# Broadcasts of source indices cut into pieces of 112, 8 and 8 partitions

## The chip, the core and the metric

The kernel runs on one core of one Trainium2 chip. The metric is the device time of one execution in microseconds, as the median of several runs. Beside it stands one execution that was taken with the hardware profiler; all views of a profile come from that one.

## The reference

One GraphSAGE layer over a random graph: 12,500 nodes with 64 features, 800,000 edges, and for each node the sum of the features of the nodes that point to it, scaled by the inverse of its degree.

```python
def reference(x, src, dst, deg_inv, w_self, w_neigh):
    N = x.shape[0]
    nsum = _segment_sum(x[src], dst, N)
    h_neigh = nsum * deg_inv[:, None]
    return x @ w_self + h_neigh @ w_neigh
```

`src` and `dst` are uniform random integers, so every node has about 64 edges, and which ones is known only at run time.

## The kernel before, in words

The kernel has no gather of single rows over the 800,000 edges. It sorts the edges into buckets on the chip and turns both the gather and the segment sum into matmuls with one-hot matrices.

**Sorting (until about 1100 us).** Each edge becomes one 32-bit key of the block of its destination (144 nodes, two halves of 72), the block of its source (128 nodes), and its places within the two. VectorE sorts 128 runs of 6,250 keys, GpSimd gathers pieces of the runs with indirect DMAs, VectorE merges them, and the result is cut into 87 x 98 = 8,526 buckets of 128 slots, one for each pair of destination and source block. This is done in two parts: 128 rows of 41 buckets first, then 128 rows of 27 (`KPRS`). The merges, the search and the decoding of the second part (lines 272 to 324, 606, 655 and 672 to 726 among others) run beside the node stage until about 1670 us. Decoding leaves two tables: `sl` in DRAM, a row of 128 bf16 source places for each bucket, and `dlT` in SBUF, the destination places, slots on the partitions.

**The node stage (`nodes`, from 1098 us to 2176 us).** All that the change touches lies here. The 8,526 buckets are taken in order, in tiles of 8:

- `one_hots` (line 770) makes the one-hot matrices for 28 buckets at a time, 305 times. A broadcast DMA from SyncE's queue (line 777) copies the 28 rows of `sl`, 7,168 bytes in one piece, to each of the 128 partitions of the tile `slb`; so a broadcast is 128 rows of 7 KB, 896 KB. VectorE compares it with the partition's number (line 779), which gives `ohs`: for each bucket a matrix of 128 source nodes by 128 slots. Line 782 compares `dlT` with 0 to 71 and gives `ohd`, slots by destinations.
- `gather` (line 798): for each bucket TensorE multiplies `ohs` with the features of the source block, `xh` (two f16 halves of each number, 128 columns), into PSUM (`ct`, line 807): the features of the 128 edges of the bucket. ScalarE copies a tile of 8 buckets to SBUF as f16 (`xg`, line 817); from tile 540 on every second one is VectorE's where the one-hots are far enough ahead (line 815).
- `sums` (line 826): TensorE multiplies `xg` with `ohd` into one of two accumulators (`acc`, line 863), 64 slots at a time. This is the segment sum. It runs two or three tiles behind `gather`.
- Every 7 destination blocks the accumulators are copied out (`g`), multiplied with `w_neigh` (`po`, line 931), scaled, added to the self terms (`fo`, an ACT-queue load of 126 partitions) and stored (`out`, GpSimd's queue). A few edges that fit in no bucket come from indirect DMAs (`lx`, line 844).

What sets the order: the loops run under a manual schedule, so each engine gets its instructions in the order in which the code is written. `gather` fetches one-hots until 44 buckets lie ahead (`AHEAD`). The tiles `slb` and `ohs` have 3 buffers each, `ohd` 6, `xg` 7 and `ct` 3: SyncE issues a broadcast when VectorE's compare has freed the buffer three broadcasts back, and the compare waits for the landing of its broadcast and for TensorE to be done with an `ohs` three back. Each DMA from SyncE or ScalarE takes one of eight completion semaphores in turn (`DMAHW0` to `DMAHW7`), and one that comes to a semaphore whose last DMA may still be under way waits for that.

The self terms, the check of the leftovers and the general path (lines 941 to 1016, which runs only if the buckets overflow) play no part in what follows.

Of the kernel before, what the change touches and what calls it, by code (L numbers as in the profile page):

```python
# [335 lines left out]
class Kernel:  # L336
# [433 lines left out]
    def one_hots(self, pool):  # L770


        nc = self.nc
        for c in range(0, NBID, 28):
            b = pool.tile([128, 28 * 128], BF, name="slb", bufs=3)
            src = self.sl[c:c + 28]
            nc.sync.dma_start(b, bass.AP(tensor=src.tensor, offset=src.offset, ap=[[0, 128], [1, 28 * 128]]))
            s = pool.tile([128, 28, 128], FH, name="ohs", bufs=3)
            nc.vector.tensor_scalar(s.rearrange("p c s -> p (c s)"), b, self.pidx[:, :1], None, op0=OP.is_equal)  # L779
            d = pool.tile([128, 14, HN, 2], FH, name="ohd", bufs=6)  # L780
            ix = self.dlT[:, c:c + 28].rearrange("p (c t) -> p c t", t=2)[:, :, None, :].to_broadcast([128, 14, HN, 2])
            nc.vector.tensor_tensor(d, self.iota[:, None].to_broadcast([128, 14, HN, 2]), ix, op=OP.is_equal)  # L782
            yield [(s[:, j], d[:, j // 2, :, j % 2]) for j in range(28)]
# [376 lines left out]
```

## Time and profile before

| | us |
|---|---|
| median of three runs | 2203.3 |
| the three runs | 2197.75, 2203.3, 2210.69 |
| the profiled execution | 2187.6 |
| its span, first to last instruction | 2185.9 |
| start of the first broadcast | 1098.1 |
| last broadcast issued | 2160.9 |
| mean granted TensorE clock | 0.769 |

Names in a profile: PE is TensorE's matmul, PEld its load of weights, DVE is VectorE, ACT ScalarE, POOL GpSimd, SP SyncE; L807 is line 807 of the kernel, and `ct<-xh,ohs` a result and its operands by the program's names. A row of the waits reads "engine, tile and line that waited <- who ended it: us in total, times, the longest". "issue" there means that the engine stood and nothing that the profile shows held it. The chain of waits is followed back from the last instruction: at each step to what released it, or to the instruction before it on its engine. A window is a stretch of the span in us. A DMA queue's row gives its packets, its megabytes, and the time that its packets took as a share of 16 DMA engines' span.

### The profile page before, as it was taken

Reading aid. Unit: us, or ns where it says so; the run is one execution under the profiler, and the core shown is the slowest. Engines: PE = TensorE matmul, PEld = TensorE weight load, DVE = VectorE, ACT = ScalarE, POOL = GpSimd, SP = SyncE. Lnnn points to the kernel's source line nnn. Section 1 sums busy time; section 2 is a strip of 40 time slices with the busy share of each in tenths; the row PEclk is TensorE's granted clock in tenths of the full one; section 3 lists DMA queues with packets and bytes.
Section 4 is the critical chain, followed back from the end, with each engine's and each line's share of the span. In section 5 each row is a group of like instructions: output and inputs, shape, how many; then the busy total and the mean of one; then the engine's idle time right before and its main releaser. Section 6 shows DMA issues by size and latency. Waiting matters only on the chain.

```text
span 2185.9 us, 59793 instructions
## 1 busy us (share of the span) xinstructions
PE 1026.7 (47%) x26089; PEld 885.7 (41%) x26089; DVE 1997.1 (91%) x2193; ACT 1263.6 (58%) x1743; POOL 648.6 (30%) x1016
## 2 busy tenths in 40 slices
PE   0050000000000000000068998999987989999888
PEld 0050000000000000000067887878776877788777
DVE  7899999999899599988999999999998988898887
ACT  6470000009700000062269999999998888898887
POOL 0000000000888888977771101011340110100110
PEclk9975555555555555555589999999999999999999
DMA  5140000001000000011177787777876787787785
GB/s 162 29 107 11 0 0 0 0 7 53 21 20 19 18 13 14 10 50 51 47 271 263 269 293 265 280 262 281 309 275 232 274 288 281 264 312 280 272 284 177
DMA packets 111471, 331.46 MB, mean 152 GB/s; under 512 B 57008, under 2 KB 65136, under 8 KB 110560
## 3 DMA queue, kind: packets, MB, share of 16 engines
q1 hardware_dynamic: 74127, 299.80, 37.0%
q0 software_dynamic: 14736, 18.99, 4.9%
q10 hardware_dynamic: 22337, 8.76, 1.8%
q8 instruction: 206, 3.38, 0.6%
q14 instruction: 65, 0.53, 0.1%
HBM read 308.39 MB, written 19.10 MB: 150 GB/s over the span
## 4 chain that ended last, share of the span: by engine, by line
PE 36%; DVE 33%; POOL 10%; issue 9%; ACT 8%; DMA 2%; ACTq 1%; another core or an unknown queue 0%; DVEq 0%; POOLq 0%; SPq 0%
PE ct L807 21%; PE acc L863 14%; DVE a L228 9%; DVE b L228 9%; POOL u L467 6%; DVE u L292 6%; ACT xg L817 3%; POOL pad L382 2%; ACT junka L448 2%; DVE u L324 2%; DMA v<-d,ix 1%; POOL v L625 1%; PE po L931 1%; DVE u L280 1%; ACT junk L604 1%
## 5 line engine op out<-in xcount | busy, mean ns | idle before, releaser
L817 ACT ACTIVATE xg<-ct 128x1024 f16<-128x1024 f32 (+1 forms) x994 | 939.1, 1091 | 99.2 <-PE ct L807 79.1
L807 PE MATMUL ct<-xh,ohs 128*128 128x128 f16 x8526 | 600.7, 221 | 58.0 <-issue 24.6
L807 PEld LDWEIGHTS <-ohs 128*128 128x128 f16 x8526 | 496.5, 99 | 104.7 <-issue 44.1
L467 POOL DMA_INDIRECT u<-d,ix x256 | 336.0, 1313 | 543.4 <-ACT junka L448 500.8
L292 DVE TENSOR_TENSOR u<-u 128x256 f32<-128x256 f32 (+47 forms) x494 | 452.8, 947 | 23.1 <-ACT u L276 15.7
L863 PE MATMUL acc<-ohd,xg 64*128 64x72 f16 x17052 | 410.1, 194 | 49.2 <-issue 35.1
L863 PEld LDWEIGHTS <-xg 64*128 64x128 f16 x17052 | 323.9, 94 | 124.6 <-issue 45.7
L779 DVE TENSOR_SCALAR ohs<-slb,pidx 128x3584 f16<-128x3584 bf16 x305 | 350.1, 1148 | 20.3 <-PE ct L807 17.1
L782 DVE TENSOR_TENSOR ohd<-iota,dlT 128x2016 f16<-128x2016 bf16 x305 | 365.8, 1199 | 0.0
L692 PE MATMUL tr<-idb,l 128*128 128x128 bf16 x68 | 9.0, 271 | 492.5 <-ACT l L686 487.6
L228 DVE TENSOR_TENSOR b<-a 128x106 f32<-128x106 f32 (+36 forms) x112 | 227.3, 2080 | 10.3 <-ACT a L231 9.3
L228 DVE TENSOR_TENSOR a<-b 128x106 f32<-128x106 f32 (+31 forms) x114 | 228.5, 2056 | 1.2
L276 ACT ACTIVATE u<-u 128x256 f32<-128x256 f32 (+15 forms) x94 | 47.3, 589 | 309.7 <-DVE u L280 308.3
L692 PEld LDWEIGHTS <-l 128*128 128x128 bf16 x68 | 5.6, 116 | 496.0 <-ACT l L686 491.4
L457 PE MATMUL stp<-idf,st 128*128 128x128 f32 x2 | 0.9, 446 | 420.4 <-DVE st L455 420.4
L939 POOL DMA_DIRECT2D out<-o x24 | 24.3, 1014 | 540.0 <-DVE o L938 470.6
L457 PEld LDWEIGHTS stp<-idf,st 128*128 128x128 f32 x2 | 0.4, 183 | 420.9 <-issue 420.9
L844 POOL DMA_INDIRECT lx<-xt,lxi x44 | 80.0, 1818 | 297.9 <-DVE lxi L842 181.0
L815 DVE CAST xg<-ct 128x1024 f16<-128x1024 f32 x75 | 91.6, 1222 | 58.1 <-PE ct L807 57.7
L231 ACT ACTIVATE a<-b 128x106 f32<-128x106 f32 (+12 forms) x20 | 13.5, 710 | 218.8 <-DVE b L228 195.2
L382 POOL MEMSET pad<- 128x89 f32 x594 | 114.6, 193 | 17.4
L625 POOL DMA_INDIRECT v<-d,ix x68 | 85.3, 1254 | 53.4 <-ACT ix L655 19.2
(134 smaller groups left out, 846.5 us busy)
## 6 DMA issues: line engine op xcount, KB each, us to landing
slb<-sl SPq DMA_DIRECT2D x305, 896.0 KB
u<-d,ix POOLq DMA_INDIRECT x256
xt<-xh SPq DMA_DIRECT2D x1, 3136.0 KB
own<-os SPq DMA_DIRECT2D x12, 256.0 KB
fo<-own ACTq DMA_DIRECT2D x24, 126.0 KB
out<-o POOLq DMA_DIRECT2D x24, 126.0 KB
rd<-dst SPq DMA_DIRECT2D x5, 521.0 KB
rs<-src SPq DMA_DIRECT2D x5, 521.0 KB
```

The source lines that it names most:

```text
L228: nc.vector.tensor_tensor(view(dst, lo + sh, [[st, g], [1, l]]), x, y, op=op)
L292: nc.vector.tensor_tensor(to, at(cur, ln + lo, n), at(cur, lo + k, n), op=op)
L382: self.nc.gpsimd.memset(self.pad, 0.0)
L467: nc.gpsimd.indirect_dma_start(out=u[:nr, p * w:(p + 1) * w], out_offset=None, in_=src, in_offset=bass.IndirectOffsetOnAxis(ap=self.start[ ...
L625: self.nc.gpsimd.indirect_dma_start(out=self.v[:, k].bitcast(F32), out_offset=None, in_=flat(self.d2[part], 128 * PITCH2[part]), in_offset ...
L779: nc.vector.tensor_scalar(s.rearrange("p c s -> p (c s)"), b, self.pidx[:, :1], None, op0=OP.is_equal)
L782: nc.vector.tensor_tensor(d, self.iota[:, None].to_broadcast([128, 14, HN, 2]), ix, op=OP.is_equal)
L807: nc.tensor.matmul(ct[:, i * 128:(i + 1) * 128], cols[i][0], self.xh[:, (b0 + i) % NB].rearrange("p a f -> p (a f)"), start=True, stop=True)
L815: nc.vector.tensor_copy(xg[:, :cnt * 128], ct[:, :cnt * 128])
L817: nc.scalar.activation(xg[:, :cnt * 128], ct[:, :cnt * 128], AF.Copy)
L844: nc.gpsimd.indirect_dma_start(out=x, out_offset=None, in_=self.xt, in_offset=bass.IndirectOffsetOnAxis(ap=ix.bitcast(U32), axis=0))
L863: nc.tensor.matmul(acc[h][:, db % OCT * HN:(db % OCT + 1) * HN], xg[r, i * 128:(i + 1) * 128], d[r], start=db % OCT == 0 and sb == 0, stop ...
```

## The change

Each broadcast is issued as three DMAs: one to partitions 0 to 111, one to 112 to 119 and one to 120 to 127. They read the same 7 KB and write the same tile. As the change is described, some DMA engines then get 9 of the 128 rows and the others 7, where each had 8.

```diff
         for c in range(0, NBID, 28):
             b = pool.tile([128, 28 * 128], BF, name="slb", bufs=3)
             src = self.sl[c:c + 28]
-            nc.sync.dma_start(b, bass.AP(tensor=src.tensor, offset=src.offset, ap=[[0, 128], [1, 28 * 128]]))
+            for p, n in ((0, 112), (112, 8), (120, 8)):
+                nc.sync.dma_start(b[p:p + n], bass.AP(tensor=src.tensor, offset=src.offset, ap=[[0, n], [1, 28 * 128]]))
             s = pool.tile([128, 28, 128], FH, name="ohs", bufs=3)
             nc.vector.tensor_scalar(s.rearrange("p c s -> p (c s)"), b, self.pidx[:, :1], None, op0=OP.is_equal)
```

The order on PE, DVE, ACT and POOL is the same in both programs; lines behind 777 are numbered one higher. On SP 305 rows become 915. The broadcasts of the first chunks as they stand on SP before, from the second and third of the stage on, each with the semaphores that it waits for (DVE frees the buffer, DMAHW is a landing):

```order
L777 DMA slb<-sl 128x3584 x2
L777 DMA slb<-sl 128x3584 [waits DMAHW0_49,DVE_49]
L777 DMA slb<-sl 128x3584 [waits DMAHW1_49,DVE_49]
L777 DMA slb<-sl 128x3584 [waits DMAHW2_49,DVE_49]
L777 DMA slb<-sl 128x3584 [waits DMAHW3_49,DVE_49]
L777 DMA slb<-sl 128x3584 [waits DMAHW4_49,DVE_49]
```

And the same place now, from the third broadcast on:

```order
L778 DMA slb<-sl 112x3584
L778 DMA slb<-sl 8x3584
L778 DMA slb<-sl 8x3584 [waits DMAHW0_49]
L778 DMA slb<-sl 112x3584 [waits DMAHW2_49,DMAHW1_49,DVE_49]
L778 DMA slb<-sl 8x3584
L778 DMA slb<-sl 8x3584 [waits DMAHW3_49]
L778 DMA slb<-sl 112x3584 [waits DMAHW5_49,DMAHW4_49,DVE_49]
L778 DMA slb<-sl 8x3584 [waits DMAHW6_49]
L778 DMA slb<-sl 8x3584 [waits DMAHW7_49]
```

The large piece waits for the buffer as the whole broadcast did; the small ones follow it at once, but mostly wait for the landing of the DMA that had their semaphore, eight issues before. On DVE the compare stands where it stood, with other waits. Before, between the merges of the second part (`u`) early in the node stage:

```order
L779 TENSOR_SCALAR ohs<-slb,pidx 128x3584 [waits DMAHW2_49,PE_49]
L782 TENSOR_TENSOR ohd<-iota,dlT 128x2016
L292 TENSOR_TENSOR u<-u 128x734
L292 TENSOR_TENSOR u<-u 128x736 [waits DVE_49]
L779 TENSOR_SCALAR ohs<-slb,pidx 128x3584 [waits DMAHW4_49,PE_49]
```

And the same rows now:

```order
L780 TENSOR_SCALAR ohs<-slb,pidx 128x3584 [waits DMAHW3_49,DMAHW4_49,DMAHW2_49,PE_49]
L783 TENSOR_TENSOR ohd<-iota,dlT 128x2016
L292 TENSOR_TENSOR u<-u 128x734
L292 TENSOR_TENSOR u<-u 128x736 [waits DVE_49]
L780 TENSOR_SCALAR ohs<-slb,pidx 128x3584 [waits DMAHW6_49,DMAHW7_49,DMAHW0_49,PE_49]
```

The compare waits for three landings in place of one; nothing else moved.

## The prediction

> **What bounds the kernel now.** I read the page first, for the DMA queues and the instruction counts. The queues' rows give packets, megabytes and the share of 16 engines' span that the packets took.
>
> ```profile
> span 2185.9 us, 59793 instructions
> PE 1026.7 (47%) x26089; PEld 885.7 (41%) x26089; DVE 1997.1 (91%) x2193; ACT 1263.6 (58%) x1743; POOL 648.6 (30%) x1016
> q1 hardware_dynamic: 74127, 299.80, 37.0%
> q0 software_dynamic: 14736, 18.99, 4.9%
> q10 hardware_dynamic: 22337, 8.76, 1.8%
> q8 instruction: 206, 3.38, 0.6%
> q14 instruction: 65, 0.53, 0.1%
> slb<-sl SPq DMA_DIRECT2D x305, 896.0 KB
> ```
>
> The broadcasts are most of the traffic: 305 x 896 KB = 279.8 MB of q1's 299.80 MB (93.3%). q1 took 37.0% of 16 x 2185.9 us, which is 12,940 us of engine time; 93.3% of it, over 305 x 128 = 39,040 rows of 7 KB, is 0.31 us a row. The other reading is of q8, "instruction": 206 packets of 16.4 KB. PE and PEld together have 52,178 instructions, so a packet is 253 of them at 64.8 bytes, and the remaining 7,615 instructions fit q14 in the same way (70 bytes each). I take q8 as PE's own program, fetched in blocks; a block took 0.6% x 16 x 2185.9 / 206 = 1.02 us.
>
> The changed line works only in the node stage, from 1098 us on. I cut it at 1670 us, where the last of the sorting work that DVE does beside it is over, and asked for the busy times of the two windows (each engine's us, with its instructions in brackets).
>
> ```profile
> core 0: us, PE busy (x) PEld busy (x) DVE busy (x) ACT busy (x) POOL busy (x), PEclk, DMA share, GB/s
> 1098.00:1670.00 572.00, 517.00 (x13227) 443.29 (x13227) 547.19 (x647) 536.79 (x637) 132.75 (x99) 0.97 0.78 275
> 1670.00:2176.00 506.00, 462.54 (x12626) 405.16 (x12626) 444.17 (x505) 433.35 (x468) 49.46 (x39) 0.99 0.77 275
> ```
>
> DMA is busy 77 to 78% as a mean of 16 engines, so bandwidth as such is not used up. PE is at 90% and 91%, DVE at 96% and 88%, ACT at 94% and 86%. No engine is full in the second window, so something outside them makes them wait. The waits of the second window name it:
>
> ```profile
> ACT xg L817 <- PE ct L807: 63.2, 110, 3.2
> DVE xg L815 <- PE ct L807: 52.8, 47, 4.2
> PE acc L863 <- issue: 20.1, 22, 2.3
> PE ct L807 <- issue: 15.8, 15, 3.1
> ```
>
> ACT and DVE wait for PE; PE waits for "issue", for nothing that the profile shows: 20.1 + 15.8 = 35.9 us in 37 waits, which is 83% of the 43.5 us that PE is idle in this window (506.00 less 462.54). One such wait in the timeline (start, length, and in brackets the idle time before it):
>
> ```profile
> 1874.67 0.70 PE L863 MATMUL acc<-ohd,xg 64*128 64x72 f16 x32
> 1875.30 0.40 PE L807 MATMUL ct<-xh,ohs 128*128 128x128 f16 x4
> 1878.78 0.84 PE L807 MATMUL ct<-xh,ohs 128*128 128x128 f16 x12 [3.08 <-issue]
> 1879.21 1.22 DVE L815 CAST xg<-ct 128x1024 f16<-128x1024 f32 x1 [4.25 <-PE ct L807]
> 1879.72 1.03 ACT L817 ACTIVATE xg<-ct 128x1024 f16<-128x1024 f32 x1 [3.19 <-PE ct L807]
> ```
>
> PE stops in the middle of a tile's sixteen matmuls, after four, with its operands there, and goes on 3.08 us later; DVE and ACT then show 4.25 and 3.19 us of waiting for it. A stop inside a run of equal matmuls, together with a program that comes in blocks of 253 instructions, I read as a block that had not arrived. That such a wait sets the end is shown by the chain of waits, cut to the second window:
>
> ```profile
> by line: PE ct L807 47.5%; PE acc L863 30.5%; issue 9.3%; PE po L931 2.3%; DVE xg L815 2.3%; DVE ohd L782 1.9%; DVE ohs L779 1.9%; ACT xg L817 1.9%; PE acc L868 1.7%; DVE o L937 0.3%; DVE ltop L726 0.2%; DVE g L873 0.1%; DVE o L938 0.1%; DV
> ```
>
> It runs through PE's matmuls and 9.3% of it is issue, 47 us. DVE and ACT are about 2% each per line. In the first window DVE has the merges beside this work, and there the waits and the chain say:
>
> ```profile
> ACT xg L817 <- PE ct L807: 15.9, 21, 2.8
> PE acc L863 <- issue: 15.0, 14, 2.7
> PE ct L807 <- issue: 8.8, 10, 1.6
> ```
> ```profile
> by line: PE ct L807 38.2%; PE acc L863 24.6%; issue 11.9%; ACT xg L817 11.5%; PE po L931 1.6%; DMA slb<-sl 1.2%; PE acc L868 1.2%; DVE ohd L782 1.2%; ACT u L276 1.1%; DMA d<-u 1.1%; DVE ohs L779 1.0%; ACT l L686 0.6%; ACT ix L655 0.6%; POOL
> ```
>
> Issue is 15.0 + 8.8 = 23.8 us in 24 waits. PE's two lines are 62.8% of that chain and issue 11.9%, but ACT's copies have 11.5%, so I let three quarters of what PE gains there reach the end.
>
> **The change part by part.** Each broadcast of 28 buckets is one DMA of 128 rows now, and becomes three of 112, 8 and 8. Bytes, tiles and buffers stay, and so does the order on PE, DVE, ACT and POOL. The split, as the change is described, gives some engines nine rows of each broadcast and the others seven.
>
> *The rows on one engine.* At 0.31 us a row, an engine now works 8 x 0.31 = 2.48 us on a broadcast; with seven rows 2.17 us, with nine 2.79 us. The issues of a broadcast are 3.50 us apart, from these rows ((2160.9 - 1098.1) / 304):
>
> ```profile
> L777 SPq DMA_DIRECT2D slb<-sl x305: 319/320/427, 1098.1 to 2160.9; - x153
> L779 DVE TENSOR_SCALAR ohs<-slb,pidx x305: 1127/1145/1335, 1102.6 to 2169.7; 128x3584 f16<-128x3584 bf16 x153
>   DMA slb<-sl: 2.7, 3
> ```
>
> That fills an engine to 71%, 62% or 80%. The two windows hold 2 x (13,227 + 12,626) = 51,706 PE and PEld instructions, 204 blocks in 1078 us, so a fetch of 1.02 us comes every 5.3 us; if all lie on one engine, they fill 19% more of it. With the broadcast's rows such an engine is at 90% now, 81% with seven rows and 99% with nine. A fetch that arrives while the engine works through its rows has to wait for them, and at 90% it mostly will.
>
> *What that is worth.* I take the fetch to get in when the engine has finished its share of one DMA. The longest waits of PE, 3.1 us, fit that: share and fetch together are 2.48 + 1.02 = 3.5 us, less whatever lead the fetch had. The share of the large DMA falls from eight rows to seven on every engine, so a fetch that waits for its end starts 0.31 us sooner and the PE wait that it causes shrinks by as much. Second window: 37 x 0.31 = 11.5 us; some waits are shorter than 0.31 us and give less, so 10.5. First window: 24 x 0.31 = 7.4 us, three quarters of it 5.5. Sum -16 us. Bounds: above, nothing (0), if the fetch isn't held by the broadcasts at all; below, half of all 59.7 us of issue waits, -30 us, if the waits shrink as those of a random queue do, with load / (1 - load): 9.0 at 90%, 4.3 at 81%. I take the one-row value: its terms are durations and counts of rows, and the broadcasts come at a steady pace, not at random.
>
> [...]
>
> *SP.* 610 more issues at 0.32 us are 195 us of SP's time, 1.0 us a broadcast instead of 0.32. What hides them:
>
> ```profile
> SPq L777 <- DVE ohs L779: 882.2, 295, 11.1
> SPq L777 <- DMA slb<-sl: 31.3, 27, 3.1
> ```
>
> SP stands for 882.2 us waiting until DVE frees a buffer, 3.0 us a broadcast, and nothing else of this stage is in its queue but the last store. So 0. Each completion semaphore now comes round after eight issues, that is 2 2/3 broadcasts, so the last piece of a broadcast waits for the first piece of the one two before it; behind it in SP's queue stands only the next broadcast, which waits for DVE longer. If that cover were gone it would be up to the 31.3 us that SP waits for landings now.
>
> *DVE.* The compare waits for three landings and PE instead of one and PE. How it stands now:
>
> ```profile
> L779 DVE TENSOR_SCALAR ohs<-slb,pidx 128x3584 f16<-128x3584 bf16 x148 | 169.6, 1146 | 4.1 <-PE ct L807 3.7
> ```
>
> With two waits it had 4.1 us idle over 148 and nearly all was PE's. The third and fourth wait lie behind 1.1 us instructions: 0, at most another 4.1 us.
>
> *Landing.* Nine rows take 0.31 us more than eight and the last piece is issued 0.64 us after the first. DVE waited for a landing 2.7 us in all, in three places, since three buffers keep the broadcasts ahead. I put 1 us on it, for the stage's first broadcast, which nothing precedes:
>
> ```profile
> 1098.49 7.12 DMA slb<-sl
> ```
>
> At most it would be 0.95 us for each of the three, 3 us. Total: -16 + 1 = -15 us.
>
> **The rivals.** *A: as above*, -15 us (0 to -30).
>
> *B: nothing moves.* The engines' work is the same bytes, and if fetches are held by something other than the rows of one broadcast (a busy memory, their own latency) the waits stay at 59.7 us. For it: DMA is only at 77%, and DVE almost never waits for a landing. Against: the waits lie in the stage with the broadcasts. Time: within 5 us of before.
>
> *C: the fetch lies on an engine with nine rows and gets in only after all three pieces.* Its share is then one row longer: 61 x 0.31 = 19 us of longer waits, and some blocks that come in time now come late too; I take +20 us. Above that the engine itself may be full. q0 and q10 took 4.9 + 1.8% of the span, 146 us of each engine, and if half of it falls beside the 305 broadcasts that is 0.24 us for each. Nine rows, the fetch's part (1.02 x 3.50 / 5.3 = 0.67) and this make 2.79 + 0.67 + 0.24 = 3.70 us a broadcast against 3.50: 305 x 0.20 = +61 us. It decides as soon as that sum passes 3.50 us. No view of before tells on which engine the fetch lies. I take half and half, and in half of the bad cases the fetch gets in behind the seven rows all the same, which would be A.
>
> [...]
>
> **How the numbers follow.** Chances: A 0.50, B 0.22, C 0.20, D 0.08. The profiled execution took 2187.6 us (its span 2185.9 and 1.7 around it), so A gives 2172.6 there; the median of the runs, 2203.3, lies 15.7 us higher (0.7%), and on it A gives 2188. About 0.5%, 11 us, is what a measurement of this kernel can tell from no change. A's values under -11 hold most of its chance: faster 0.45. Same: B and the small end of A, 0.28. Slower: C and D, 0.27. Range: down to A's bound, 2203.3 - 30 = 2173; up to C's taken value and a little, 2203.3 + 23 = 2226. Left out are D and the upper part of C, under 2 in 10.
>
> **What would show it.** Right: the issue waits of PE in the two windows fall from 59.7 us towards 44, their number hardly, and the "xg" waits of ACT and DVE for PE fall with them; SP still mostly waits for DVE. C: the issue waits grow past 75 us. [...] Wrong altogether: the issue waits halve and the time stays, or the time moves with the issue waits unchanged.

## The result, and the profile after

The changed kernel takes 2451.4 us (median of 4 runs, 2436.0 to 2453.8) where the kernel before takes 2200.5 us in the same comparison: a ratio of 1.110, 95% interval 1.106 to 1.114. The prediction was 2188 us with a range up to 2226. It was wrong in sign and by 263 us in size.

The page of the profile after, its span and the queues of the broadcasts and of PE's instruction blocks:

```profile
span 2452.1 us, 60712 instructions
...
q1 hardware_dynamic: 79007, 299.82, 48.4%
...
q8 instruction: 206, 3.38, 0.7%
```

The packets are what the change says (4,880 more: 305 x 16 packets of 4 bytes, which I read as completions), the megabytes are the same, and q1 takes 48.4% of the span instead of 37.0%. By the prediction's own working, with 93.3% of it for the broadcasts, a row of 7 KB now costs 0.484 x 16 x 2452.1 x 0.933 / 39,040 = **0.454 us** instead of 0.31. The records of the single packets of 7,168 bytes in the two traces agree: 0.455 us in the mean, and 0.303 before. The node stage (from 1098 us on, cut at its middle; columns as in the prediction) shows it too:

```profile
1098.00:1770.00 672.00, 534.94 (x12794) 462.18 (x12795) 535.22 (x616) 526.05 (x612) 92.99 (x95) 0.88 0.91 227
1770.00:2440.00 670.00, 526.76 (x13005) 459.49 (x13006) 468.02 (x536) 453.94 (x491) 44.59 (x43) 0.89 0.89 215
```

The mean DMA engine is busy 91% and 89% now, not 78% and 77%, and moves 227 and 215 GB/s instead of 275: busier with less. SP's issues on the changed line (minimum, median and maximum ns, first and last start) give the pace:

```profile
L778 SPq DMA_DIRECT2D slb<-sl x915: 263/308/1902, 1098.1 to 2424.1; - x183
```

Between broadcasts lie (2424.1 - 1098.1) / 304 = 4.36 us. If a row costs the same on every engine, nine of them take 9 x 0.454 = 4.09 us, which leaves such an engine next to nothing for other work. Who waits in this stage (us in total, times, longest):

```profile
ACT xg L818 <- PE ct L808: 296.1, 232, 12.8
...
DVE ohs L780 <- DMA slb<-sl: 141.3, 112, 3.9
...
PE acc L864 <- issue: 100.1, 64, 5.1
...
DVE xg L816 <- PE ct L808: 74.9, 42, 4.7
...
PE ct L808 <- issue: 58.9, 31, 4.1
```

DVE's waits for landings are 141.3 us instead of 2.7, and PE's for instruction blocks 100.1 + 58.9 = 159.0 us instead of 59.7. That these are waits for blocks can be read from the packets of q8 themselves: before, 52 of the 57 waits over 0.2 us end 1.1 to 1.7 us after such a packet has ended (median 1.43), now 84 of 94 end 1.2 to 2.0 us after one (median 1.53). SP, which stood behind DVE for 882.2 us and behind landings for 31.3, now shows:

```profile
SPq L778 <- DVE ohs L780: 502.3, 290, 8.6
...
SPq L778 <- DMA slb<-sl: 352.3, 379, 4.2
```

C's mark, issue waits past 75 us, is there. But the waits for landings have grown too, to 141.3 us on DVE and 352.3 us on SP, and C's mark says nothing of them, so it alone doesn't show the cause. The stage is 1342 us instead of 1078, 264 more. On PE, 82 of these are its own busy time (534.94 + 526.76 = 1061.7 against 979.5), at a granted clock of 0.88 and 0.89 where it was 0.97 and 0.99. Another 99 are waits for instruction blocks. The rest is nearly all longer waiting for DVE and ACT.

### The profile page after: what moved, and what is told of

Same layout as the page of the kernel before. It is cut to its first block, busy times and chain, and to the rows that moved or that the text cites. A ratio compares the mean times of both kernels' runs of the same rounds, so it can differ in the third digit from the quotient of the medians.

```text
span 2452.1 us, 60712 instructions
## 1 busy us (share of the span) xinstructions
PE 1110.6 (45%) x26089; PEld 960.3 (39%) x26089; DVE 2009.4 (82%) x2193; ACT 1274.8 (52%) x1743; POOL 604.8 (25%) x1016
## 3 DMA queue, kind: packets, MB, share of 16 engines
q1 hardware_dynamic: 79007, 299.82, 48.4%
## 4 chain that ended last, share of the span: by engine, by line
DMA 26%; DVE 23%; PE 18%; POOL 17%; issue 11%; ACT 5%; ACTq 1%; SPq 0%; DVEq 0%; POOLq 0%
DMA slb<-sl 14%; POOL u L467 12%; PE ct L808 10%; DVE a L228 8%; DVE b L228 8%; DMA fo<-own 8%; PE acc L864 7%; POOL pad L382 4%; ACT junka L448 2%; DVE ohs L780 2%; POOL v L625 1%; DMA v<-d,ix 1%; ACT xg L818 1%; DVE ohd L783 1%; DVE u L292 1%
## 5 line engine op out<-in xcount | busy, mean ns | idle before, releaser
L808 PE MATMUL ct<-xh,ohs 128*128 128x128 f16 x8526 | 654.7, 233 | 142.6 <-issue 58.9
L808 PEld LDWEIGHTS <-ohs 128*128 128x128 f16 x8526 | 544.8, 105 | 193.9 <-issue 95.9
L864 PE MATMUL acc<-ohd,xg 64*128 64x72 f16 x17052 | 434.5, 201 | 137.8 <-issue 100.1
L780 DVE TENSOR_SCALAR ohs<-slb,pidx 128x3584 f16<-128x3584 bf16 x305 | 352.1, 1154 | 175.5 <-DMA slb<-sl 141.3
L467 POOL DMA_INDIRECT u<-d,ix x256 | 322.8, 1261 | 543.0 <-ACT junka L448 500.5
L864 PEld LDWEIGHTS <-xg 64*128 64x128 f16 x17052 | 347.5, 99 | 216.9 <-issue 130.5
L845 POOL DMA_INDIRECT lx<-xt,lxi x44 | 55.6, 1263 | 415.2 <-PE ct L808 233.4
```

Source lines behind the costliest of these rows:

```text
L467: nc.gpsimd.indirect_dma_start(out=u[:nr, p * w:(p + 1) * w], out_offset=None, in_=src, in_offset=bass.IndirectOffsetOnAxis(ap=self.start[ ...
L808: nc.tensor.matmul(ct[:, i * 128:(i + 1) * 128], cols[i][0], self.xh[:, (b0 + i) % NB].rearrange("p a f -> p (a f)"), start=True, stop=True)
L845: nc.gpsimd.indirect_dma_start(out=x, out_offset=None, in_=self.xt, in_offset=bass.IndirectOffsetOnAxis(ap=ix.bitcast(U32), axis=0))
L864: nc.tensor.matmul(acc[h][:, db % OCT * HN:(db % OCT + 1) * HN], xg[r, i * 128:(i + 1) * 128], d[r], start=db % OCT == 0 and sb == 0, stop ...
```

## The experiments

Most of these kernels differ from the change in its two lines alone (the loop and its `dma_start`), and the diffs show what stands there in each. Ratios are to the kernel before on the same chip, with 95% intervals. "Row" is the engine time of one 7 KB row, worked out from q1's share as above. Between two runs with the same broadcasts it differed by 0.01 us (0.31 before, 0.32 in the run of fewer buffers below), so smaller differences say nothing.

### Is it the number of DMAs, or the partitions?

**24, 2 and 2 buckets.** Three DMAs as in the change, but cut by columns, all 128 partitions in each:

```diff
+for p, n in ((0, 24), (24, 2), (26, 2)):
+    nc.sync.dma_start(b[:, p * 128:(p + n) * 128],
+                      bass.AP(tensor=src.tensor, offset=src.offset + p * 128, ap=[[0, 128], [1, n * 128]]))
```

> Three DMAs for each broadcast again, so the same 915 issues, completions and semaphore waits, but each to all 128 partitions: 24, 2 and 2 of the 28 buckets. [...] Theory N (three DMAs instead of one cost it: issues, completions, semaphores that come round sooner): slow as after, 1.08 to 1.12, with SP waiting some 350 us for landings. Theory H (the engines with nine rows are full): as before, 0.98 to 1.01.

2210.9 us, ratio 1.004 (1.001 to 1.007).

```profile
span 2200.2 us, 60712 instructions
...
q1 hardware_dynamic: 161967, 299.84, 39.8%
```
```profile
PE acc L865 <- issue: 46.1, 51, 2.3
...
PE ct L809 <- issue: 26.6, 26, 2.8
...
DVE ohs L781 <- DMA slb<-sl: 4.1, 2, 3.5
```

The issues, the completions and the semaphores of the change cost next to nothing: 0.4%. Issue waits are 72.7 us: a shorter share of the large DMA did not shorten them.

**112 and 16.** By count every engine has eight rows (seven and one):

```diff
+for p, n in ((0, 112), (112, 16)):
```

> Two DMAs, 112 and 16 partitions: by counts each of 16 engines then has seven and one rows, eight as before. [...] Theory N: in between, 1.03 to 1.06. Theory H: no engine has nine rows, so as before, 0.99 to 1.01.

2430.3 us, ratio 1.101 (1.097 to 1.105).

```profile
span 2434.6 us, 60249 instructions
...
q1 hardware_dynamic: 79007, 299.82, 47.2%
```
```profile
PE acc L864 <- issue: 144.3, 76, 4.4
...
PE ct L808 <- issue: 81.4, 41, 5.0
```

Row 0.472 x 16 x 2434.6 x 0.933 / 39,040 = 0.44 us with equal shares and two DMAs. The shares are by count, and the trace names no engine. The packets fit them: q1 has as many as with the change (79,007), so sixteen rows in one DMA add the 16 packets a broadcast that two times eight rows add there. Nine tenths of the loss are there without an engine of nine rows. It reaches PE by 225.7 us of issue waits this time; I read them as fetches that stand behind slower rows. C's mark thus appears without the nine rows that C is about.

**Eight extra rows, near and far.** The kernel before, with one more DMA of 8 rows x 6.5 KB a broadcast into a tile that nobody reads, once to partitions 0 to 7, once to 0, 4, ..., 28 (`ohd` 5 and `xg` 6 buffers, to make room):

```diff
+x = pool.tile([128, 26 * 128], BF, name="slx", bufs=1)
+nc.sync.dma_start(x[:8], bass.AP(...))        # near
+nc.sync.dma_start(x[0:32:4], bass.AP(...))    # far
-d = pool.tile([128, 14, HN, 2], FH, name="ohd", bufs=6)
+d = pool.tile([128, 14, HN, 2], FH, name="ohd", bufs=5)
-xg = pool.tile([128, 1024], FH, name="xg", bufs=7)
+xg = pool.tile([128, 1024], FH, name="xg", bufs=6)
```

> The broadcast whole, as before, and behind it an extra DMA of eight rows of 6.5 KB to partitions 0 to 7 of a tile that nothing reads (to make room, 5 buffers for the destination one-hots instead of 6, 6 for the gathered rows instead of 7). [...] Theory H: eight engines have nine rows, as in after: 1.05 to 1.12, and the same as with the extra rows spread. Theory N: 1.02 to 1.05, the same with the rows spread.

> As the run with extra rows to partitions 0 to 7, but to partitions 0, 4, 8 and so on to 28: the same bytes, rows, engines by count, issues and waits, no two rows for neighbours. [...] Theories H and N: the same as that run within 0.01.

Near: 2212.6 us, 1.002 (0.998 to 1.005). Far: 2193.8 us, 0.995 (0.992 to 0.998). The fewer buffers by themselves, as zero point:

> The kernel before with the buffer counts of the two runs with an extra DMA (ohd 5, xg 6) and no extra DMA, to have their zero point. If the two buffers are worth nothing: within 0.3% of before, and the extra eight rows cost 0 to +0.5%. If fewer buffers themselves bring the 0.5% of the run with the spread rows: 2185 to 2198 us.

2200.6 us, 1.000 (0.998 to 1.003). N had put the near run at 1.02 or more, H at 1.05 or more. H, the nine rows, falls with it: by count eight engines have nine rows here too, and that costs 0.2% (0.5% at the end of its interval) in the near run and nothing in the far one. By the packets of 6.5 KB in the traces an extra row takes 0.37 us near and 0.31 us far. A small piece on neighbouring partitions thus costs 14 us more than a spread one by the ratios (0.0065 of 2204), 19 us by the medians. Why the far run is 0.5% faster than its zero point is open.

This prices a small piece beside whole broadcasts, whose rows are quick, and no compare waits for the extra tile. It has one buffer, so that SP waits for the landing of the last extra piece, here near and then far:

```profile
SPq L779 <- DMA slx<-sl: 730.7, 289, 4.7
```
```profile
SPq L779 <- DMA slx<-sl: 440.1, 259, 5.0
```

So twice this price, some 28 to 38 us, is no more than a hint of what the change's two small pieces cost beside a slow large one.

**112 alone.** One DMA, 112 partitions; the kernel leaves out the other 16 source nodes of each bucket, in the compare and the matmul too:

```diff
+nc.sync.dma_start(b[:112], bass.AP(..., ap=[[0, 112], [1, 28 * 128]]))
```

> One DMA of 112 partitions a broadcast and nothing for the other 16; the compare and the gather matmul use 112 partitions, so the kernel leaves out 16 of the 128 source nodes of each bucket and moves 12.5% fewer broadcast bytes. [...] Rival S (the small second piece or the pair of pieces is what costs, the large piece is as quick as before): row 0.31 us, seven rows 2.2 us, time 2165 to 2195 us, issue waits under 50 us.

2259.2 us, 1.023 (1.016 to 1.029), with an eighth fewer broadcast bytes than before.

```profile
span 2256.6 us, 59794 instructions
...
q1 hardware_dynamic: 69247, 264.82, 40.9%
```

The broadcasts are 244.8 of these 264.82 MB (92.4%): 0.409 x 16 x 2256.6 x 0.924 / 34,160 = 0.40 us a row. The large piece itself is slow, and PE's issue waits are 98.9 us, so rival S is out. But this kernel is only 51 us slower than before, and with the other sixteen rows it is 2430.3: how the loss in time divides between the large piece and the small ones isn't shown.

### Which partitions

**126 and 2.** This was meant as the harmless uneven cut:

```diff
+for p, n in ((0, 126), (126, 2)):
```

> Pieces of 126 and 2 partitions: by count fourteen engines have nine rows and two have one. [...] Rival U (any large piece of other than 128 partitions is slow, or nine rows on an engine are): row 0.42 us or more, time over 2400 us.

2402.8 us, 1.088 (1.080 to 1.096): the time that U had, but not its row.

```profile
span 2403.3 us, 60249 instructions
...
q1 hardware_dynamic: 74127, 299.80, 42.9%
```

Row 0.39 us: about as with 112 alone, far from 0.31. So this cut wasn't harmless, and no run shows why. q1's packets are as many as before (74,127), so the two DMAs together have the 16 packets of 4 bytes a broadcast that the one had; that fits fourteen engines and two. No trace shows which engines get the last two rows: if two of the fourteen, these have ten.

**64 + 64, halves against even and odd.** The same counts, rows, bytes and rows per engine:

```diff
+for p, n in ((0, 64), (64, 64)):  nc.sync.dma_start(b[p:p + n], ...)
+for p in (0, 1):                  nc.sync.dma_start(b[p::2], ...)
```

> [...] Rival U (any piece of other than 128 partitions): over 2400 us.

> Two pieces of 64 partitions as in the run of 64 + 64, but the even and the odd partitions instead of the lower and the upper half: the same count of DMAs, rows, bytes and rows per engine. [...] Rival U (a DMA of other than 128 rows is slow whatever it writes): row 0.50 us or more, time over 2500 us.

Halves: 2562.4 us, 1.161 (1.154 to 1.169).

```profile
span 2561.8 us, 60252 instructions
...
q1 hardware_dynamic: 79007, 299.82, 52.3%
```
```profile
PE acc L864 <- issue: 188.8, 89, 5.0
...
PE ct L808 <- issue: 129.7, 52, 5.3
```

Even and odd: 2209.2 us, 1.003 (1.000 to 1.006).

```profile
span 2203.4 us, 60252 instructions
...
q1 hardware_dynamic: 79007, 299.82, 39.8%
```
```profile
PE acc L864 <- issue: 39.6, 43, 2.6
PE ct L808 <- issue: 36.2, 33, 2.2
```

Row 0.51 us against 0.34, issue waits 318.5 us against 75.8. Only the partitions that a DMA writes differ. That shows the kind of cause: which partitions a DMA writes sets the price of its rows, 0.51 us or 0.34 here. How it comes about, no run shows.

**4 x 32, neighbours against steps of 4.** The same comparison with four pieces:

```diff
+for p in (0, 32, 64, 96):  nc.sync.dma_start(b[p:p + 32], ...)
+for p in range(4):         nc.sync.dma_start(b[p::4], ...)
```

> [...]

> [...]

Neighbours: 2497.1 us, 1.136 (1.130 to 1.142), row 0.51 us.

```profile
span 2493.5 us, 61156 instructions
...
q1 hardware_dynamic: 88767, 299.86, 53.3%
```

Steps of 4: 2183.9 us, 0.993 (0.990 to 0.995). The same kernel measured again:

> The kernel of four DMAs of 32 partitions in steps of 4 once more, in more rounds, since it came out 0.7% faster than before in one. If that was real: ratio 0.990 to 0.996 and PE's issue waits 40 to 50 us. If it was the scatter of that chip or hour: ratio 0.997 to 1.003.

2187.0 us (12 runs), 0.993 (0.991 to 0.995): real, as both runs have it, with issue waits of 39.6 us.

```profile
span 2184.6 us, 61158 instructions
...
q1 hardware_dynamic: 88767, 299.86, 41.8%
```
```profile
PE acc L864 <- issue: 21.8, 32, 2.3
...
PE ct L808 <- issue: 17.8, 36, 1.1
```

So 32 neighbours cost what 64 do (0.51 us a row), and 32 partitions in steps of 4 about what 64 in steps of 2 do (0.35 against 0.34). The trace doesn't show which engine writes which partition, so why that is stays open, and so does how 112 rows are given out.

### What the shares themselves cost

**Spread, nine and seven.** The change's shares from pieces of 64 even and 48, 8 and 8 odd partitions:

```diff
+for p, e, n in ((0, 128, 64), (1, 96, 48), (97, 112, 8), (113, 128, 8)):
+    nc.sync.dma_start(b[p:e:2], ...)
```

> The change's uneven shares without its blocks of neighbours: four DMAs a broadcast, of 64 even partitions (four rows on each engine), 48 odd ones (three), 8 odd and 8 odd ones (one more row on each of eight engines, twice), so that by count eight engines have nine rows and eight have seven, as in the change. Theory P (the change is slow because of which partitions its pieces write): row 0.31 to 0.36 us, time 2195 to 2265 us, of which the uneven shares are what is above the 2209 of 64 even + 64 odd. Rival H (the nine rows themselves are a large part of the change's 250 us): time over 2330 us, with PE's issue waits over 120 us. If A of the prediction holds once the blocks of neighbours are gone (seven rows on the engine of the fetches): issue waits under 50 us.

2367.3 us, 1.075 (1.071 to 1.080): the time where rival H had it, but issue waits of 97.1 us (56.3 + 40.8), not over 120.

```profile
span 2370.6 us, 61155 instructions
...
q1 hardware_dynamic: 83887, 299.84, 47.5%
```

Row 0.43 us against 0.34 with all the odd partitions in one piece: the pieces of 48 and 8 have slow rows too, and the run doesn't price the shares. The next pair does it better, with steps over all partitions:

```diff
+(0, 128, 2, 64), (1, 128, 4, 32), (3, 128, 8, 16), (7, 128, 8, 16)             # equal: start, end, step, rows
+(0, 128, 2, 64), (1, 128, 4, 32), (3, 128, 8, 16), (7, 64, 8, 8), (71, 128, 8, 8)   # nine and seven
```

> [...] Rival N4 (four DMAs a broadcast are what made the run of spread 9 and 7 slow): row over 0.40 us, time over 2330 us.

> [...] Against the run above it prices the uneven shares alone. Theory S (shares cost what C of the prediction put on nine rows): +10 to +61 us, 2205 to 2290 us, row under 0.36 us. Rival H (nine rows on an engine are the larger part of the change's 250 us): over 2330 us. If A of the prediction holds with the neighbours kept apart: issue waits under 50 us and a time under the run above.

Equal: 2227.0 us, 1.014 (1.009 to 1.018). Nine and seven: 2266.8 us, 1.033 (1.027 to 1.038). Rows 0.37 and 0.36 us, a little over the 0.34 of even and odd; N4 is out, and so is H. Their waits, the equal one first:

```profile
PE ct L808 <- issue: 37.0, 34, 3.0
PE acc L864 <- issue: 36.2, 40, 2.8
...
DVE ohs L780 <- DMA slb<-sl: 25.6, 24, 3.0
```
```profile
DVE ohs L780 <- DMA slb<-sl: 100.4, 89, 4.4
...
PE acc L864 <- issue: 12.3, 12, 2.3
...
PE ct L808 <- issue: 7.7, 12, 1.9
```

The uneven shares cost some 40 us at most, as the fifth DMA is in that. PE's issue waits fall from 73.2 to 20.0 us, under A's 44, while DVE's waits for landings rise from 25.6 to 100.4 us. The engines with nine rows may be behind that, but so may SP, which with five issues of 0.567 us has hardly any time left in which it waits for DVE (167.1 us in the equal run, 882.2 before):

```profile
SPq L778 <- DVE ohs L780: 26.2, 26, 5.6
```

Whether the fetches gained because their engine has seven rows, or because PE waits for DVE meanwhile, this pair doesn't tell.

### What the fetches cost, and smaller shares

**No broadcasts** after the first three, whose tiles are used for all (the source indices are stale):

```diff
+if c < 84:
+    b = pool.tile([128, 28 * 128], BF, name=f"slb{c // 28}", bufs=1)
...
+b = held[c // 28 % 3]
```

> Only the first three broadcasts are made and their tiles are used again for all others, so the source indices are those of the first 84 buckets. It shows what of PE's issue waits the broadcasts cause. If the broadcasts hold the instruction blocks up: issue waits fall from about 60 us to under 20 us and the time to 2140 to 2165 us. If the blocks are late by themselves: 50 to 60 us of issue waits stay, 2185 to 2205 us.

2138.7 us, 0.969 (0.963 to 0.975), 1.3 us under the range expected.

```profile
PE acc L867 <- issue: 1.9, 5, 0.5
```
```profile
q8 instruction: 206, 3.38, 0.7%
```

Of the issue waits on PE's two lines 1.9 us are left, with as many instruction blocks fetched (206). So the broadcasts do hold the blocks up, as the prediction read from the timeline, and 69 us, by which the time falls, is the most that is to be had from it. Without the broadcasts PE had 5 such waits for 206 blocks; beside them it had 61 before and 95 with the change.

**14 and 14 buckets**, all partitions, half the share per DMA:

```diff
+for p, n in ((0, 14), (14, 14)):
+    nc.sync.dma_start(b[:, p * 128:(p + n) * 128], ...)
```

> Each broadcast as two DMAs of all 128 partitions, 14 buckets each, so that an engine's share of one DMA is half as long and ends twice as often. Theory A of the prediction (a waiting instruction block gets in when the engine has finished its share of one DMA): the share falls from 2.5 to 1.25 us, PE's issue waits from about 60 to 25 to 40 us, time 2165 to 2190 us. Theory R (a block waits behind the rows queued on its engine, of whichever DMA, as the run of 24, 2 and 2 buckets suggested): issue waits 55 to 80 us, time 2195 to 2220 us.

2235.0 us, 1.014 (1.011 to 1.018).

```profile
PE acc L865 <- issue: 71.1, 66, 3.3
...
PE ct L809 <- issue: 40.7, 36, 2.3
```

111.8 us of issue waits: more, not less, and outside both expectations; why is open.

**One row per DMA**, eight DMAs of 16 partitions in steps of 8:

```diff
+for p in range(8):
+    nc.sync.dma_start(b[p::8], bass.AP(..., ap=[[0, 16], [1, 28 * 128]]))
```

> Eight DMAs of 16 partitions in steps of 8, one row on each engine. If a waiting instruction block gets in between DMAs, so that smaller shares free PE: issue waits under 47 us (those of steps of 4) and a time no more than 2200 us as long as SP keeps up (8 x 0.32 = 2.6 us of issues in 3.5). If the number of DMAs ahead counts (a semaphore comes round after eight issues, now one broadcast): SP waits for landings, DVE waits for them over 100 us, time over 2260 us.

2830.1 us, 1.286 (1.280 to 1.292). The issues (minimum, median and maximum ns, first and last start), and DVE:

```profile
L778 SPq DMA_DIRECT2D slb<-sl x2440: 471/587/2145, 1098.3 to 2812.1; - x188
```
```profile
DVE ohs L780 <- DMA slb<-sl: 635.1, 259, 7.6
```

SP is the bound here: its issues of stepped partitions take 0.587 us, 4.7 us a broadcast at the median, and it waits for landings for 1.2 us in all. I had reckoned 2.6 us, though the run of steps of 4 had shown 0.592 us an issue by then. It says nothing on the fetches, since PE mostly waits for DVE. But it has a row:

```profile
span 2829.7 us, 62943 instructions
...
q1 hardware_dynamic: 108287, 299.94, 37.2%
```

0.372 x 16 x 2829.7 x 0.933 / 39,040 = 0.40 us, as slow as in the piece of 112, though each piece lies over all of the 128 partitions and the mean DMA engine is busy for only 63% of the stage (1098 to 2812 us). So an even spread alone doesn't make a row cheap.

## Why the prediction was wrong

**The failing step is the first: "Bytes, tiles and buffers stay", with "At 0.31 us a row".** The row's price was taken over from a DMA of 128 partitions to pieces of 112 and 8, as if it belonged to the bytes. It belongs to the DMA's partitions: 0.31 us (128), 0.40 (112 alone), 0.44 (112 and 16), 0.454 (the change). If a row costs the same on every engine, seven then cost 3.18 us and nine 4.09, not 2.17 and 2.79; the engine of seven rows is busy for 73% of a broadcast (3.18 of 4.36 us), where that of eight was for 71%. The terms of A, C and landing stood on this price; those of SP and DVE did not.

**A, the shorter share (-16 us).** Its premise is right: without broadcasts the issue waits go. Its quantity isn't borne out: 72.7 us with 24 buckets, 75.8 with shares of four rows, 111.8 with half the buckets, and clearly less only in steps of 4 (47.2 and 39.6) and in two runs in which PE waits for DVE instead (20.0 with the uneven spread, 12.1 with one row per DMA). The term assumed that a block waits for the end of one DMA's share; the column cuts speak against that. Why four DMAs in steps of 4 gain 13.6 us, near the 20 us by which the issue waits fall, is open.

**D, rows for neighbouring partitions that get in each other's way (0.08).** No run shows how such rows would hold each other up, nor what a row of the two pieces of eight takes. What the runs show in its place is a price for each cut: 0.51 us a row for 64 neighbours against 0.34 for every second partition, 0.40 for 112 alone, 0.454 for the change. So D had the direction, and too small a chance. If the rows of 112 keep their 0.40 us beside the small pieces, the sixteen other rows take (128 x 0.454 - 112 x 0.40) / 16 = 0.83 us each, and the added engine time divides about 55 to 45 between the large piece and the small ones. This is an estimate, and no run measures the two side by side. No broadcast of before is cut into pieces of 112 or 8. That should have made the row's price an open cost with a wide bound, since all rows of before are of one kind and the trace had no other.

**C, nine rows (+20 to +61).** The cleanest pair gives at most 40 us, and the extra rows next to nothing. It fits as a size, but as a part of 251 it is small: 112 and 16, with equal shares, already has 1.101 of the 1.110.

**Landing (+1 us)** failed with the row: 141.3 us on DVE. **SP (0)** held as far as the issues go: 915 of them, cut by columns, cost 0.4%. **DVE (0)** held in the same run, where the compare waits for three landings and shows 4.1 us.

**The second-order loss.** PE's own 82 us of longer busy time had no term. The granted clock over the whole span fell from 0.769 to 0.741 here, and was lowest in the two longest runs: 0.737 with the two halves, 0.717 with one row per DMA. I read the lower clock as a consequence of the waits, but no experiment separated the two.

## What to carry to other kernels

Before cutting a DMA by partitions, ask which partitions each piece writes: the rows of a DMA over all 128 (0.31 us), or in steps of 2 or 4 over all of them (0.34 and 0.35), were cheap here, those of sixteen in steps of 8 (0.40) were not, and those of a run of 32 or 64 neighbours (0.51) cost up to two thirds more than 0.31. The check is one row of the page, the queue's share times engines and span over its rows, and it belongs ahead of any working on queues. A price that the trace shows in one shape only is unknown in another, and its bound must hold that.

## What the runs showed of the hardware

- The row of 7 KB: 0.31 us (128 partitions), 0.34 (even and odd), 0.35 (steps of 4), 0.39 (126 and 2), 0.40 (112 alone, and sixteen in steps of 8), 0.44 (112 and 16), 0.454 (112, 8, 8), 0.51 (64 or 32 neighbours).
- SP's issue, at the median: 0.320 us for the 128 rows of before, 0.419 for 32 neighbours and 0.592 for 32 in steps of 4, 0.527 for 64 neighbours and 0.556 for 64 in steps of 2, 0.587 for 16 in steps of 8.
- PE goes on some 1.4 us after the packet of an instruction block that it waited for has ended (before, median of 52 waits).
- Four DMAs of 32 partitions in steps of 4 are faster than either kernel, by little: 2187.0 us, 0.993 of before (0.991 to 0.995).
